# A fused adaLN block on one core: a new start-up order, another bound for the projection's scale, and operations that the planner deals between two engines

## The chip, the cores and the metric

The kernel runs on one core of one Trainium2 chip. TensorE (PE) multiplies, VectorE (DVE), ScalarE (ACT) and GpSimd (POOL) work on what it needs and leaves, and SyncE (SP) issues all the transfers from one queue. The metric is the time of one execution on the device, in microseconds (us). The program is the same each time; three executions of it are given below.

## The reference, cut to what matters

x is 2048 rows of 512. There are 32 heads of 128, and each query sees the last 512 rows of the cache (W), so that attention is over 512 keys for every one of the 2048 queries, without a mask.

```python
mod = (silu(c) @ w_mod).reshape(...)            # six vectors of 512: sa, ca, ga, sb, cb, gb
h = layernorm(x) * (1 + ca) + sa
q = h @ wq                                      # 32 heads of 128
p = softmax(q @ k.T * Dh ** -0.5)               # k, v: the last 512 rows of the cache
x = x + ga * ((p @ v) @ wo)
h = layernorm(x) * (1 + cb) + sb
x = x + gb * ((gelu(h @ w_gate) * (h @ w_up)) @ w_down)      # 512 -> 1376 -> 512
```

All inputs are float32.

## The kernel before, in words

**Precision.** Every large product is made of f16 matmuls. An operand is split in two f16 parts, high and low (`in_two`: ScalarE copies to f16, GpSimd subtracts that copy from the float32 value), and three products of 128x128 by 128x512 stand for one. So that the parts fit f16, each weight tile is multiplied by a power-like scale taken from its largest absolute value (`h_max`, then `cross_a` and `cross_b`, which bring eight such maxima across the partitions with a transpose and a small matmul and take a reciprocal), and the columns that scale and shift the first LayerNorm are multiplied by one factor (`cols_bound`, `cols_scale`), which `s_scale` takes out again in the softmax's scale.

**The work.** 16 groups of two heads, each with 4 blocks of 512 queries: 128 iterations of one head and one block (`slot`). An iteration makes scores `s_mm` (12 matmuls into `psS`), their row maxima `s_max` on VectorE, exponentials `s_exp` on ScalarE (into `p`, then an f16 copy `pp`), the low part `s_low` on GpSimd and its transposition by DMA (`pT`), the product with v `pv` (`psO`), its split `oT`, the product with wo (`psW`) and its addition into `acc`, in all 36 matmuls; the query projection (`psQ`) of a later iteration comes between. Beside that run the loads, scalings and splits of the next group's weights, and one time LayerNorm (`ln_stats`, `ln_norm`, then `chunk`: four transposes of 128x128 into PSUM, `ln1_split`: scale and shift, high part, low part). After the last group comes the feed-forward part; the last groups' iterations carry its first preparation (LayerNorm 2: `ln2_norm`, `ln2_chunk`, `ln2_high`, `ln2_low`; sums for a Strassen-like scheme: `f_full`, `f_sum`, `f_low`, `aw_sum`).

**The order.** Nothing is issued where it is written. A class `Weaver` stands in front of the engines: `note` records each operation with its engine, its planned duration and what it depends on, and `issue` then plans. It takes a due time for each operation from the order of the matmuls (`rank`), plays the program forward with a list scheduler (`play`: at each moment the engine that is free takes, among the operations that are ready, the one with the earliest due time), plays it backward for new due times (`back`), repeats this `TURNS` times, keeps the order with the earliest end and issues it. Each engine then works in that order and waits by semaphores for what its next operation needs. All instructions are issued from one line, `real(*a, **k)`, line 314; so nearly every instruction in the profile has L314, and only its tiles tell operations apart.

`play` also knows a port that GpSimd and VectorE have in common: each GpSimd operation, and each VectorE operation of the kind marked `lock` (a `tensor_scalar`, or one with two large operands in SBUF), holds it to its end. Each operation has one fixed engine, written into the code.

**The start.** `PLAN` lists by hand the steps of the start, and so the due times of the matmuls: those with -1 come before the first iteration, the others hang at halves of iterations. The loads are noted as x's first four tiles (`load_x(0)`), `wq` and `k` of head 0, `w_mod`'s two quarters-of-columns for the scale and the shift (`load_mod(1)`, `load_mod(0)`, four transfers of 256 KB each), then more of x and of the weights; the planner orders them. `stats`, `norm`, `turn0` and `chunk` make the first normalised block. `mod` (`mod_mm`, 4 matmuls with one column each for each of the 8 pieces of w_mod) makes the modulation columns in PSUM (`two`), `cols_add` adds them up, `cols_bound` takes

```python
nc.vector.tensor_tensor(sq, cols[:, 0:8], cols[:, 0:8], op=OP.mult)
nc.tensor.matmul(two[:, 0, 16:24], ones, sq, start=True, stop=True)
nc.vector.tensor_reduce(sc1[:, 2:3], two[:, 0, 16:24], op=OP.add, axis=AX.X)
```

and a power of -1/2 on GpSimd, `cols_scale` multiplies. `warm` (54, 0, 0, 2, 1, 16, 0 times) transposes the identity into a PSUM bank of its own (`warmed`, a `psQ`), with nothing read from it.

Of the kernel before, what the change touches and what calls it, by code (L numbers as in the profile page):

```python
# [17 lines left out]
P = 128  # L18
# [32 lines left out]
    (-1, "stats", 0, 0), (-1, "stats", 0, 1), (-1, "stats", 0, 2), (-1, "warm", 54), (-1, "stats", 0, 3),  # L51
    (-1, "mod", 1, 0), (-1, "mod", 1, 1), (-1, "max", "first", 0), (-1, "norm", 0, 2, "V"), (-1, "max", "first", 1),
    (-1, "mod", 1, 2), (-1, "cross", "first", "a"), (-1, "warm", 0), (-1, "mod", 1, 3), (-1, "norm", 0, 3, "V"),
    (-1, "warm", 0), (-1, "cross", "first", "b"), (-1, "mod", 0, 0), (-1, "high", "k", 0), (-1, "turn0", 3),
    (-1, "mod", 0, 1), (-1, "norm", 0, 1, "V"), (-1, "norm", 0, 0, "V"), (-1, "mod", 0, 2), (-1, "turn0", 2),
    (-1, "mod", 0, 3), (-1, "warm", 2), (-1, "low", "k", 0), (-1, "stats", 1, 0), (-1, "cols_add"),
    (-1, "cols_bound"), (-1, "stats", 1, 1), (-1, "turn0", 0), (-1, "high", "wq", 0), (-1, "cols_scale"),
    (-1, "s_scale"), (-1, "stats", 1, 2), (-1, "warm", 1), (-1, "scalars", 0, "qk"), (-1, "turn0", 1),
    (-1, "warm", 16), (-1, "low", "wq", 0), (-1, "max", "second", 1), (-1, "chunk", 0, 0, "", "S", "Y"),
    (-1, "max", "second", 0), (-1, "chunk", 0, 1, "", "S", "Y"), (-1, "warm", 0), (-1, "chunk", 0, 2, "", "V", "V"),  # L60
    (-1, "chunk", 0, 3, "", "S", "V"), (-1, "q", 0), (-1, "q_high", 0), (-1, "turn", 0), (-1, "stats", 1, 3),
# [24 lines left out]
class Weaver:  # L86


    LAG, DRAIN, LANES, TURNS = 60.0, 165.0, 8, 6
    NEXT = {"ACT": 95.0, "DVE": 85.0, "POOL": 45.0, "PE": 0.0, "SP": 0.0}  # L90

    def __init__(self, nc):
        self.nc = nc
        for name, engine in (("vector", "DVE"), ("scalar", "ACT"), ("gpsimd", "POOL"), ("tensor", "PE"), ("sync", "SP")):
            setattr(self, name, self.Port(self, engine, getattr(nc, name)))
        self.ops, self.held, self.seen, self.before, self.rings, self.table = [], {}, {}, {}, {}, {}
# [55 lines left out]

    def note(self, engine, what, real, a, k):
        op = len(self.ops)
# [4 lines left out]
        for x, write in [(x, False) for x in read] + [(x, True) for x in wrote]:  # L159
# [4 lines left out]
            if held is None:  # L164
                continue
# [23 lines left out]
        self.ops.append((engine, d, deps, real, a, k, n, lock))  # L189

    def rank(self):
# [18 lines left out]
        for engine, d, *_ in self.ops:  # L210
            at.append(t if engine == "PE" else 1e12)
            t += d if engine == "PE" else 0.0
# [7 lines left out]
    def play(self, at, users):  # L220
# [4 lines left out]
        can = {e: [] for e in self.NEXT}  # L225
        for n, op in enumerate(self.ops):
            if not op[2]:
                heapq.heappush(wait[op[0]], (0.0, n))
        free, landed, bus, shared, order = {e: 0.0 for e in self.NEXT}, [], 0.0, 0.0, []
        ends = [0.0] * len(self.ops)  # L230
        while len(order) < len(self.ops):
            t, e = min((max(free[e], 0.0 if can[e] else wait[e][0][0]), e) for e in free if can[e] or wait[e])
            while wait[e] and wait[e][0][0] <= t:
                n = heapq.heappop(wait[e])[1]
                heapq.heappush(can[e], (at[n], n))
            aside = []
            if e == "DVE" and shared > t + 100.0:
                while can[e] and self.ops[can[e][0][1]][7]:
                    aside.append(heapq.heappop(can[e]))
                if not can[e] and wait[e] and wait[e][0][0] < shared:  # L240
                    free[e] = wait[e][0][0]
            pick = None if aside and free[e] > t else heapq.heappop(can[e]) if can[e] else aside.pop(0)
            for x in aside:
                heapq.heappush(can[e], x)
            if pick is None:
                continue
            n = pick[1]
            order.append(n)
            d, size, lock = self.ops[n][1], self.ops[n][6], self.ops[n][7]
# [13 lines left out]
            for m in users[n]:  # L263
                ready[m] = max(ready[m], t + d if e == "PE" == self.ops[m][0] else end)
                left[m] -= 1
                if not left[m]:
                    heapq.heappush(wait[self.ops[m][0]], (ready[m], m))
        return order, ends

    def back(self, ends, users):  # L270
# [5 lines left out]
        for n, op in enumerate(self.ops):  # L276
            if not users[n]:
                heapq.heappush(wait[op[0]], (0.0, n))
        free, shared, done, at = {e: 0.0 for e in self.NEXT}, 0.0, 0, [0.0] * len(self.ops)
        while done < len(self.ops):  # L280
# [6 lines left out]
            d, size, lock = self.ops[n][1], self.ops[n][6], self.ops[n][7]  # L287
            if e == "SP":
                d = max(d, size)
# [5 lines left out]
            for m in self.ops[n][2]:  # L295
                f = self.ops[m][0]
# [3 lines left out]
                if not left[m]:  # L300
                    heapq.heappush(wait[self.ops[m][0]], (ready[m], m))
        return at

    def issue(self):
        at, users = self.rank()
        best = None
        for _ in range(self.TURNS):
            order, ends = self.play(at, users)
            if best is None or max(ends) < best[0]:
                best = max(ends), order  # L310
            at = self.back(ends, users)
        for n in best[1]:
            real, a, k = self.ops[n][3:6]
# [4 lines left out]
def adaln_block(ctx: ExitStack, tc: tile.TileContext, x, k_cache, v_cache, wq, wo,  # L318
# [83 lines left out]
    def ln_stats(key, src, j):  # L402
# [6 lines left out]
        if j == 3:  # L409
# [3 lines left out]
            if key != 0:  # L413
                nm = NMR[key] = small(base, 4, 4, "nmr")
                nc.gpsimd.tensor_tensor(nm, MV[key][:, :, 0], RS[key], op=OP.mult)
                nc.gpsimd.tensor_scalar(nm, nm, -1.0, 1.0, op0=OP.mult, op1=OP.mult)
# [70 lines left out]
    for h in range(G):  # L487
        load_raw("v", h)
        load_raw("wo", h)
    load_x(2)  # L490
    load_x(3)

# [17 lines left out]
    def h_gate(h):  # L510
        nc.gpsimd.tensor_tensor(RAW["wo", h], RAW["wo", h], ga, op=OP.mult)
# [103 lines left out]
    def a_sum(g, nm):  # L615
# [8 lines left out]
        nc.gpsimd.tensor_tensor(out, x, y, op=op)  # L624
# [4 lines left out]
    def t_full(p, c, nm, eng):  # L629
# [3 lines left out]
        eng.tensor_tensor(t, b[:, 0, c, :], b[:, 1, c, :], op=OP.add)  # L633

    def t_sum(p, c, out, x, y):
        nc.gpsimd.tensor_tensor(TF[p, c, out], TF[p, c, x], TF[p, c, y], op=OP.subtract)
# [155 lines left out]
    warmed = bank("psQ")  # L792


    def warm(n):
        for _ in range(n):
            nc.tensor.transpose(warmed[:, :P], ident, ident)

    def ln1_split(qg, c, full, low):
# [4 lines left out]
        if full is nc.scalar:  # L806
            nc.scalar.activation(f, pt, AF.Identity, scale=a, bias=b)
            nc.scalar.activation(dh, f, AF.Copy)
        else:
            nc.scalar.activation(dh, pt, AF.Identity, scale=a, bias=b)  # L810
            nc.vector.tensor_scalar(f, pt, a, b, op0=OP.mult, op1=OP.add)
        low.tensor_tensor(dl, f, dh, op=OP.subtract)
# [29 lines left out]
    sq = small(base, 8, 1, "sq")  # L842
# [795 lines left out]
```

## Time and profile before

| | us |
|---|---|
| median of 3 executions | 1701.87 |
| lowest, highest | 1700.04, 1704.01 |
| the execution that was profiled | 1702.24 |
| its span, first to last instruction | 1700.10 |
| its mean granted TensorE clock | 0.992 |
| TensorE busy | 1671.3 |
| VectorE, ScalarE, GpSimd busy | 1315.3, 1174.4, 1238.5 |

In the profile a row of a group reads: line, engine, operation, out <- in with the shapes, count, then busy time in all and nanoseconds of one, then the time that the engine stood idle just before, with what ended it. A row of the timeline reads: start, duration, engine, line, operation, out <- in, and in brackets the idle time ahead of it. A row of a stretch reads: from:to, its length, the busy time and count of each engine, the clock granted to TensorE (1.00 is full), the share of the DMA engines and GB/s. A float32 matmul of `mod_mm` leaves two records. Ends of matmuls are modelled: a 128x512 f16 matmul is shown with 380 ns, while in a dense run six of them start in 1.29 us.

### The profile page before, as it was taken

To read this page: it belongs to the slowest core of one execution; us is meant where nothing else is said; L and a number is where in the kernel's file an instruction comes from. 1 tells how busy PE (TensorE), PEld (TensorE's weight loads), DVE (VectorE), ACT (ScalarE), POOL (GpSimd) and SP (SyncE) were. 2 spreads that over 40 slices of the span, in tenths; PEclk is the share of its full clock that TensorE was granted. 3 is DMA by queue.
4 is the path that set the end of the run, shared out by engine and by line. 5 is a ranking of instruction groups with operands and counts; after the bars stand their busy time and mean duration, and the time that the engine had idled before them with its cause. 6 is when DMAs were issued, how large, how long until landed. Compare 5 with 4: busy or idle time off the path is not lost. (4 is left out here: it accounts for less than half of the span.)

```text
span 1700.1 us, 24167 instructions
## 1 busy us (share of the span) xinstructions
PE 1671.3 (98%) x7807; PEld 774.4 (46%) x7807; DVE 1315.3 (77%) x2423; ACT 1174.4 (69%) x2346; POOL 1238.5 (73%) x1033
## 2 busy tenths in 40 slices
PE   8899999999999999999999999999999999999998
PEld 6444444444444444444444444444444444444444
DVE  5887777788888777777777788888777888965665
ACT  3877777777777867777777776776777976654541
POOL 2899995878698868686777788897887786643630
PEclk7999999999999999999999999999999999999999
DMA  6777788799888878686777675787768711110011
GB/s 198 144 143 148 134 161 148 153 187 184 185 163 181 144 137 145 128 155 118 143 128 146 124 155 111 161 175 149 142 135 140 146 34 38 47 43 19 16 50 50
DMA packets 666351, 217.12 MB, mean 128 GB/s; under 512 B 581552, under 2 KB 648112, under 8 KB 666224
## 3 DMA queue, kind: packets, MB, share of 16 engines
q1 hardware_dynamic: 666224, 215.57, 63.8%
q8 instruction: 62, 1.02, 0.2%
q14 instruction: 65, 0.53, 0.1%
HBM read 68.68 MB, written 4.19 MB: 43 GB/s over the span
## 5 line engine op out<-in xcount | busy, mean ns | idle before, releaser
L314 POOL TENSOR_TENSOR pp<-p,pp 128x1024 f16<-128x1024 f32 x256 | 547.8, 2142 | 170.5 <-ACT pp L314 143.3
L314 ACT ACTIVATE p<-psS,st,es 128x512 f32<-128x512 f32 x512 | 393.2, 772 | 150.3 <-DVE st L314 129.1
L314 PE MATMUL psW<-wo,oT 128*128 128x512 f16 x1536 | 433.9, 380 | 0.3 <-DVE acc L314 0.2
L314 PE MATMUL psS<-kT,q 128*128 128x512 f16 x1536 | 418.6, 380 | 1.5 <-ACT q L314 1.3
L314 DVE SCALAR_TENSOR_TENSOR acc<-psW,st,acc 128x512 f32<-128x512 f32 x496 | 359.8, 743 | 53.6 <-PE psW L314 51.0
L314 PE MATMUL psO<-pT,v 128*128 128x512 f16 x1536 | 400.1, 379 | 0.5 <-DVE oT L314 0.5
L314 DVE TENSOR_REDUCE st<-psS 128x2 f32<-128x1024 f32 x256 | 312.0, 1219 | 79.1 <-PE psS L314 77.0
L314 ACT ACTIVATE pp<-p 128x1024 f16<-128x1024 f32 x256 | 269.8, 1054 | 10.3 <-DMA pT<-pp 5.5
L314 PEld LDWEIGHTS <-v 128*128 128x128 f16 x1536 | 150.4, 98 | 182.4 <-issue 1.9
L314 PEld LDWEIGHTS <-q 128*128 128x128 f16 x1536 | 149.8, 98 | 181.9 <-ACT q L314 4.1
L314 PEld LDWEIGHTS <-oT 128*128 128x128 f16 x1536 | 149.1, 98 | 176.6 <-issue 2.0
L314 DVE SCALAR_TENSOR_TENSOR oT<-psO,oT 128x512 f16<-128x512 f32 x128 | 87.7, 685 | 75.6 <-ACT oT L314 75.1
L314 PE MATMUL psQ<-B,A 128*128 128x512 f16 x528 | 144.2, 380 | 1.8 <-DVE A L314 1.8
L314 PEld LDWEIGHTS <-aw 128*128 128x128 f16 (+1 forms) x840 | 84.3, 100 | 96.7 <-issue 0.4
L314 PE MATMUL psQ<-T,S 128*128 128x512 f16 x468 | 115.4, 379 | 1.7 <-ACT h L314 1.7
L314 PEld LDWEIGHTS <-A 128*128 128x128 f16 x756 | 73.2, 98 | 96.2 <-issue 10.1
L314 PE MATMUL psS<-T,aw 128*128 128x512 f16 (+1 forms) x480 | 115.7, 379 | 0.0
L314 POOL TENSOR_SCALAR raw<-raw,av 128x512 f32<-128x512 f32 x122 | 85.1, 709 | 39.7 <-DVE av L314 27.5
L314 DVE TENSOR_REDUCE mx<-raw 128x1 f32<-128x512 f32 x128 | 85.9, 673 | 30.4 <-DMA raw<-in_A_v_cache_dram 18.3
L314 POOL TENSOR_TENSOR q<-h,q 128x512 f16<-128x512 f32 x78 | 90.6, 1162 | 19.3 <-ACT q L314 19.0
L314 ACT ACTIVATION_READ_ACCUMULATOR p<-psS,st,es 128x1 f32 x512 | 100.4, 196 | 0.0
L314 ACT ACTIVATE oT<-psO 128x512 f16<-128x512 f32 x128 | 75.6, 591 | 30.3 <-PE psO L314 29.9
(207 smaller groups left out, 2243.8 us busy)
## 6 DMA issues: line engine op xcount, KB each, us to landing
raw<-in_A_wq_dram SPq DMA_DIRECT2D x32, 256.0 KB, 3.4
raw<-in_A_k_cache_dram SPq DMA_DIRECT2D x32, 256.0 KB, 3.4
raw<-in_A_v_cache_dram SPq DMA_DIRECT2D x32, 256.0 KB, 3.4
raw<-in_A_wo_dram SPq DMA_DIRECT2D x32, 256.0 KB, 3.0
pT<-pp SPq DMA_TRANSPOSE x512, 3.3
raw<-in_B_w_gate_dram SPq DMA_DIRECT2D x24, 256.0 KB, 3.1
raw<-in_B_w_up_dram SPq DMA_DIRECT2D x24, 256.0 KB, 3.2
raw<-in_B_w_down_dram SPq DMA_DIRECT2D x20, 256.0 KB, 3.0
```

The costliest lines, as they stand in the source:

```text
L314: real(*a, **k)
```

## The change

1. **Loads.** x's first two groups of four tiles are noted first, then the two parts of w_mod, then k and wq of head 0, then the third group of x, and so on; and SyncE issues all of these in the order in which they are noted. Later loads are not planned sooner than 40 us (`EARLY`) before they are due.
2. **The scale.** `cols_bound` takes the sum of absolute values of the columns, in place of the sum of squares and its root: an upper bound of the same quantity, made with one column less work on TensorE and without GpSimd.
3. **Warming transposes.** 50 at the start, then 6 behind each of the eight modulation steps, now into the same PSUM tile as the modulation products (`two`).
4. **Dealing.** `either` records an operation with several possible engines, and `play` gives it to one: two-operand tensor operations (`tt`) to GpSimd or VectorE, scalings to GpSimd or ScalarE, norms and scale-and-shift from PSUM to ScalarE or VectorE. An engine leaves it if the other could end it sooner (`sooner`; a VectorE operation that needs the common port is charged `SHY` = 1500 ns more), and it also leaves any operation if one whose due time is over `WORTH` = 5000 ns earlier becomes ready before this one would be done (`pressing`).
5. **The planner.** It plans half clock for TensorE after a window of 3413 ns in which it is busy less than 35%, not counting one-column products, and takes 10 turns in place of 6.
6. The first LayerNorm also gets the column that ScalarE needs for a norm (`nmr`, two small GpSimd operations).

```diff
 PLAN = (
-    (-1, "stats", 0, 0), (-1, "stats", 0, 1), (-1, "stats", 0, 2), (-1, "warm", 54), (-1, "stats", 0, 3),
-    (-1, "mod", 1, 0), (-1, "mod", 1, 1), (-1, "max", "first", 0), (-1, "norm", 0, 2, "V"), (-1, "max", "first", 1),
...
+    (-1, "stats", 0, 0), (-1, "stats", 0, 1), (-1, "stats", 0, 2), (-1, "stats", 0, 3), (-1, "warm", 50), (-1, "mod", 1, 0), (-1, "warm", 6), (-1, "mod", 1, 1), (-1, "warm", 6),
+    (-1, "mod", 1, 2), (-1, "warm", 6), (-1, "mod", 1, 3), (-1, "warm", 6),
+    (-1, "mod", 0, 0), (-1, "warm", 6), (-1, "mod", 0, 1), (-1, "warm", 6),
+    (-1, "mod", 0, 2), (-1, "warm", 6), (-1, "mod", 0, 3), (-1, "warm", 6),
+    (-1, "cols_add"), (-1, "cols_bound"),
+    (-1, "max", "first", 0), (-1, "max", "first", 1), (-1, "cross", "first", "a"),
+    (-1, "cross", "first", "b"), (-1, "norm", 0, 0, "V"), (-1, "norm", 0, 1, "V"), (-1, "norm", 0, 2, "V"),
+    (-1, "norm", 0, 3, "V"), (-1, "turn0", 0), (-1, "turn0", 1), (-1, "turn0", 2), (-1, "turn0", 3),
+    (-1, "cols_scale"), (-1, "s_scale"), (-1, "high", "k", 0), (-1, "low", "k", 0), (-1, "high", "wq", 0),
...
-    LAG, DRAIN, LANES, TURNS = 60.0, 165.0, 8, 6
+    LAG, DRAIN, LANES, TURNS, SPAN, SHY, EARLY, WORTH = 60.0, 165.0, 8, 10, 3413.0, 1500.0, 40000.0, 5000.0
...
+        def arrive(n):
+            if span and n >= self.lead:
+                ready[n] = max(ready[n], span + at[n] - self.EARLY)
+            for e in self.ops[n][4]:
+                heapq.heappush(wait[e], (ready[n], n))
+
+        def sooner(n, e, t):
+
+            kinds = self.ops[n][4]
+            mine = max(t, shared if kinds[e][1] else 0.0) + kinds[e][0] + (e == "DVE" and kinds[e][1]) * self.SHY
+            for o, kind in kinds.items():
+                s = max(free[o], ready[n], shared if kind[1] else 0.0)
+                if o != e and s + kind[0] + (o == "DVE" and kind[1]) * self.SHY < mine:
+                    return max(s, t) + 1.0
+            return None
...
-                heapq.heappush(can[e], (at[n], n))
+                heapq.heappush(can[e], (n - 1e12 if e == "SP" and n < self.lead else at[n], n))
...
+            if e == "PE":
+                while t >= close:
+                    cold, work, close = work < 0.35 * self.SPAN, 0.0, close + self.SPAN
+                work += 0.0 if size == 1 else d
+                d *= 1.0 + cold
...
     load_x(0)
-    load_raw("wq", 0)
-    load_raw("k", 0)
+    load_x(1)
     load_mod(1)
     load_mod(0)
-    load_x(1)
+    load_raw("k", 0)
+    load_raw("wq", 0)
+    load_x(2)
     load_raw("wq", 1)
     load_raw("k", 1)
...
+    nc.lead = len(nc.ops)
...
     def h_scale(kind, h):
         raw = RAW[kind, h]
-        nc.gpsimd.tensor_scalar(raw, raw, AV[kind, h], 1.0, op0=OP.mult, op1=OP.mult)
+        av = AV[kind, h]
+        nc.either((nc.gpsimd, nc.scalar), lambda o: o.activation(raw, raw, AF.Copy, scale=av) if o is nc.scalar
+                  else o.tensor_scalar(raw, raw, av, 1.0, op0=OP.mult, op1=OP.mult))
 
     def in_two(t, src):
         nc.scalar.activation(t[:, 0, :], src, AF.Copy)
-        nc.gpsimd.tensor_tensor(t[:, 1, :], src, t[:, 0, :], op=OP.subtract)
+        tt(t[:, 1, :], src, t[:, 0, :], OP.subtract)
...
-    warmed = bank("psQ")
     def warm(n):
         for _ in range(n):
-            nc.tensor.transpose(warmed[:, :P], ident, ident)
+            nc.tensor.transpose(two[:, 1, :P], ident, ident)
+    crossing = bank("psQ")
+    def tt(out_, x_, y_, op, order=(nc.gpsimd, nc.vector)):
+        nc.either(order, lambda o: o.tensor_tensor(out_, x_, y_, op=op))
+
+    def affine(f, pt, a, b):
+        nc.either((nc.scalar, nc.vector), lambda o: o.activation(f, pt, AF.Identity, scale=a, bias=b) if o is nc.scalar
+                  else o.tensor_scalar(f, pt, a, b, op0=OP.mult, op1=OP.add))
...
-        nc.vector.tensor_tensor(sq, cols[:, 0:8], cols[:, 0:8], op=OP.mult)
+        nc.vector.tensor_reduce(sc1[:, 2:3], cols[:, 0:8], op=OP.add, axis=AX.X, apply_absolute_value=True)
     def cols_bound():
-        nc.tensor.matmul(two[:, 0, 16:24], ones, sq, start=True, stop=True)
-        nc.vector.tensor_reduce(sc1[:, 2:3], two[:, 0, 16:24], op=OP.add, axis=AX.X)
-        nc.vector.tensor_scalar(sc1[:, 3:4], sc1[:, 2:3], 1e-30, 2.0 / HQS ** 2, op0=OP.max, op1=OP.mult)
-        nc.gpsimd.tensor_tensor(sc1[:, 0:1], sc1[:, 3:4], eps_t[:, NC:NC + 1], op=OP.pow)
+        nc.tensor.matmul(two[:, 0, 16:17], ones, sc1[:, 2:3], start=True, stop=True)
+        nc.vector.tensor_scalar(sc1[:, 3:4], two[:, 0, 16:17], 1e-30, 1.0 / HQS, op0=OP.max, op1=OP.mult)
+        nc.vector.reciprocal(sc1[:, 0:1], sc1[:, 3:4])
...
     def acc_gate(t, eng):
-        eng.tensor_tensor(acc[t], acc[t], ga, op=OP.mult)
+        tt(acc[t], acc[t], ga, OP.mult)
...
     def ln2_low(qg, c, eng):
         hi, lo = f_view(qg, c)
         full = FULL.pop((qg, c)) if qg % 2 == 0 else FULL[qg, c]
-        eng.tensor_tensor(lo, full, hi, op=OP.subtract)
+        tt(lo, full, hi, OP.subtract)
```

The same replacement by `tt` stands in `h_gate`, `a_sum`, `t_full`, `t_sum`, `ln1_split`, `mod_mul`, `x_add`, `f_full`, `f_sum`, `f_low`, `wd_gate`, `plain_part`, and that of a scaling by `either` in `gu_scale` and `aw_scale`. `s_low`, `hid_low` and the sums `aw_sum` and `aw_low` of the feed-forward weights stay on their engines.

More of the change, by code (lines that the diff above doesn't have):

```diff
@@ L163, in note @@
             held = self.held.get(key)
-            if held is None:
+            if held is None or write and self.joins:
                 continue
@@ L266, in play, with back @@
                 if not left[m]:
-                    heapq.heappush(wait[self.ops[m][0]], (ready[m], m))
-        return order, ends
-    def back(self, ends, users):
+                    arrive(m)
+        return order, ends, by
+    def back(self, ends, by, users):
         import heapq
@@ L805, in ln1_split @@
         dh, dl = h_view(qg, c)
[L806 to L812, printed above, removed]
+        affine(f, pt, a, b)
+        nc.scalar.activation(dh, f, AF.Copy)
+        tt(dl, f, dh, OP.subtract)
     def ln1_turn(qg, c, where):
```

169 lines of the change are left out of this document (102 added, 67 removed).

## The prediction

> **What bounds the kernel now.** I read the page first, then busy time by stretches, the timeline of the first 40 us, what TensorE waited for, and the two places in the body where its busy time dips.
>
> ```profile
> span 1700.1 us, 24167 instructions
> ...
> PE 1671.3 (98%) x7807; PEld 774.4 (46%) x7807; DVE 1315.3 (77%) x2423; ACT 1174.4 (69%) x2346; POOL 1238.5 (73%) x1033
> ...
> 100.00:200.00 100.00, 100.00 (x466) 45.25 (x465) 74.16 (x148) 74.96 (x152) 99.17 (x77) 1.00 0.79 149
> ```
>
> TensorE is busy for 98% of the span at full clock, even between 100 and 200 us, where GpSimd (POOL) is busy for 99.17 of 100 us. No edit touches the products of attention or of the feed-forward part. So only time in which TensorE stands, or runs at half clock, can be won; nearly all of it lies in the first 70 us and at two places later.
>
> The start, from the timeline:
>
> ```profile
> 8.56 2.74 PE L314 MATMUL psS<-silu,wm 128*128 128x1 f32 x24
> ...
> 11.16 4.43 PE L314 MATMUL psQ<-ident 128*128 128x128 f32 x25
> ...
> 23.18 0.17 DVE L314 TENSOR_TENSOR cols<-psS,plus 128x8 f32<-128x8 f32 x1 [1.43 <-PE psS L314]
> ...
> 25.60 0.43 PE L314 MATMUL psS<-sq,ones 128*128 128x8 f32 x2
> ...
> 28.20 0.22 DVE L314 TENSOR_SCALAR cols<-cols,sc 128x8 f32<-128x8 f32 x1
> ...
> 28.51 0.78 ACT L314 ACTIVATE h<-psO,cols 128x512 f32<-128x512 f32 x1 [8.90 <-DVE cols L314]
> ...
> 37.42 1.24 PE L314 MATMUL psQ<-B,A 128*128 128x512 f16 x5
> ...
> 39.42 1.90 PE L314 MATMUL psS<-kT,q 128*128 128x512 f16 x8 [0.53 <-ACT q L314]
> ```
>
> The chain is: modulation products end, columns summed (23.18), a bound from their squares, columns scaled (28.20), four chunks of normalised x made (28.51 on), first projection done (38.66), first scores at 39.42. From 23.18 to 28.51 are 5.3 us of small steps, from 28.51 to 38.66 are 10.2 us for four chunks. The clock and DMA in the same stretch:
>
> ```profile
> 0.00:5.00 5.00, 3.65 (x17) 3.65 (x18) 1.10 (x4) 1.49 (x2) 1.35 (x16) 1.00 0.54 138
> 5.00:10.00 5.00, 5.00 (x46) 5.00 (x44) 1.08 (x2) 0.00 (x0) 0.00 (x0) 1.00 0.99 335
> ...
> 5.60:9.00 3.40, 3.40 (x34) 1.00 0.96 325
> 9.00:12.40 3.40, 3.40 (x32) 1.00 1.06 376
> 12.40:15.80 3.40, 3.40 (x18) 0.50 1.07 394
> 15.80:19.20 3.40, 2.94 (x26) 1.00 1.06 358
> 19.20:22.60 3.40, 3.40 (x19) 0.50 1.13 249
> ...
> 29.40:32.80 3.40, 0.94 (x2) 0.51 0.00 0
> 32.80:36.20 3.40, 3.40 (x12) 0.50 0.01 2
> ```
>
> (In the two 5 us rows the engines are PE, PEld, DVE, ACT, POOL; in the others PE alone; then clock, DMA share, GB/s.) The granted clock changes in steps of 3.4 us: a stretch of transposes (5.6 to 9.0) is followed by full clock, one of mostly one-column modulation products (9.0 to 12.4, 15.8 to 19.2) by half clock. The first real products, 29.4 to 36.2, run at half.
>
> **Part 1: the modulation chain.** New order of loads: c, 8 tiles of x, then w_mod. The two 5 us rows have moved 0.69 + 1.68 = 2.37 MB by 10 us; x's 8 tiles are 2.10 MB, so the first w_mod quarter lands at about 10.0 instead of before 8.56; the other seven follow at 0.7 us each, faster than they are used. Fifty warming transposes fill TensorE until about 9. Then eight steps of four products and six transposes, all in one PSUM tile, so in this order. Four products are 8 records: 2.74/24 x 8 = 0.91 us at full clock, 3.4/19 x 8 = 1.43 at half; six transposes 6 x 3.4/34 = 0.60, at half 6 x 3.4/18 = 1.13. A step is 1.51 or 2.56 us. All at full clock the eight take 12.1 us, and the 16 transposes of x 1.6 more: 10.1 + 13.7 = 23.8. All at half from 12.4 on: 1.5 steps done, 6.5 x 2.56 + 16 x 0.19 = 19.7, so 32.1. Transposes are 40% of a step; between 9.0 and 12.4 they were from 11.16 on, 1.2 of 3.4 us (36%), and that was not enough. I take one 3.4 us window at half (it costs 1.7): 25.5. Against 23.18 that is **+2.3** (ends +0.6 and +8.9).
>
> **Part 2: the scale.** The square, the 8-column matmul followed by a reduction, and the power on GpSimd become one absolute sum, a one-column matmul, one multiply and a reciprocal on VectorE. By the rows, 0.17 for each small step: 0.17 + 0.17 + 0.43 + 0.17 + 0.17 + 0.22, with a quarter microsecond of hand-overs, is 1.6 us, against 28.51 - 23.18 = 5.3: **-3.7**. The old chain also stood behind LayerNorm work in VectorE's and GpSimd's queues; that work now finds its x landed before it. If it comes back between the steps, 2 us of this go (end -1.7).
>
> **Part 3: the four chunks.**
>
> ```profile
> 28.72 0.20 POOL L314 TENSOR_TENSOR nmr<-mv,rs 128x4 f32<-128x4 f32 x1
> 29.01 0.27 POOL L314 TENSOR_SCALAR nmr<-nmr 128x4 f32<-128x4 f32 x1
> 31.23 1.16 POOL L314 TENSOR_TENSOR T<-h,T 128x512 f16<-128x512 f32 x1 [1.95 <-ACT T L314]
> ...
> L314 ACT ACTIVATE T<-h 128x512 f16<-128x512 f32 x3 | 1.8, 634 | 0.0
> ...
> 28.50:39.40 10.90, 7.03 (x30) 3.73 (x29) 9.33 (x26) 9.06 (x15) 6.67 (x11) 0.69 0.01 2
> ```
>
> VectorE and ScalarE were 9.33 and 9.06 of 10.9 us busy there, much of it with statistics, norms and maxima of later tiles. With x's first 8 tiles landed at 9.3 us this goes into their idle time ahead of the chunks. What is left: one affine (0.78), one f16 copy (0.63), then four subtractions on GpSimd, 4 x 1.16, and 0.4 for the last products: 6.4 us against 10.2: **-3.7** (ends 0 and -4.5). Two more GpSimd operations for the first LayerNorm (0.20 + 0.27 us) lie under the wait for w_mod; without that cover they cost 0.5.
>
> **Part 4: filling the pipeline.**
>
> ```profile
> 39.40:50.00 10.60, 7.89 (x36) 3.37 (x37) 9.41 (x23) 9.69 (x18) 6.16 (x7) 1.00 0.34 78
> 50.00:60.00 10.00, 7.26 (x32) 3.43 (x31) 8.60 (x17) 7.74 (x16) 9.67 (x9) 0.84 0.78 159
> 60.00:70.00 10.00, 8.41 (x42) 4.00 (x40) 8.97 (x17) 8.37 (x17) 6.13 (x6) 0.99 0.72 154
> ...
> PE psQ L314 <- DVE A L314: 1.8, 1, 1.8
> ...
> PE psO L314 <- DVE acc L314: 1.4, 1, 1.4
> ```
>
> TensorE idles 2.7 + 2.7 + 1.6 = 7.0 us, waiting for weight splits and for norms in VectorE's queue (the longest wait 1.8, the fourth 1.4). The 7.3 MB up to the last tile of x land by some 24 us at the 0.36 MB a us of the rows 9.0 to 19.2, so the norms can be done before. The exponentials and splits stay. I take half, **-3.5** (ends 0 and -7.0).
>
> **Part 5: the operations dealt out.** A two-operand subtraction may now go to GpSimd or VectorE. The planner's own sum charges VectorE 0.68 + 1.5 us (SHY) and GpSimd 1.16, and lets VectorE in only when the common port is free, which is when GpSimd is free too. So it deals all of them to GpSimd, VectorE's old ones among them:
>
> ```profile
> L314 DVE TENSOR_TENSOR T<-hf,T 128x512 f16<-128x512 f32 x12 | 19.8, 1660 | 1.9 <-ACT T L314 1.9
> ...
> L314 DVE TENSOR_TENSOR acc<-acc,ga 128x512 f32<-128x512 f32 x8 | 12.9, 1616 | 0.0
> ...
> L314 POOL TENSOR_TENSOR acc<-acc,ga 128x512 f32<-128x512 f32 x8 | 10.6, 1330 | 8.8 <-DVE iv L314 6.5 <-DVE acc L314 2.2
> ...
> 1038.15 6.60 DVE L314 TENSOR_TENSOR acc<-acc,ga 128x512 f32<-128x512 f32 x1
> ...
> 1374.44 7.05 DVE L314 TENSOR_TENSOR T<-hf,T 128x512 f16<-128x512 f32 x1 [1.92 <-ACT T L314]
> ...
> 1040.00:1050.00 10.00, 6.39 (x24) 2.39 (x23) 9.96 (x11) 2.49 (x6) 6.01 (x5) 0.83 0.56 105
> ...
> 1374.00:1388.00 14.00, 11.02 (x47) 4.81 (x46) 13.49 (x11) 9.90 (x18) 8.75 (x11) 0.88 0.13 39
> ...
> 1360.00:1400.00 40.00, 37.02 (x175) 17.66 (x174) 32.18 (x41) 29.46 (x52) 33.58 (x44) 0.96 0.13 37
> ...
> raw<-in_A_wq_dram SPq DMA_DIRECT2D x32, 256.0 KB, 3.4
> ```
>
> Two VectorE subtractions stretch to 6.60 and 7.05 us, while GpSimd works without a gap, and TensorE then stands 3.6 and 3.0 us and runs one 3.4 us window at half clock each: about 5.3 + 4.7 = 10 us. On GpSimd such an operation has its 1.3 us. But from 1360 to 1400 GpSimd is at 33.6 of 40 us, and some twelve moved operations bring 14 more; part of the delay returns there. I take half, **-5** (ends 0 and -10). Scalings that move to ScalarE, and loads held until 40 us before they are due, cost nothing: the first leaves GpSimd, the second has 40 us of cover for a landing of 3.4 us (the last row); without that cover each costs its landing.
>
> [...]
>
> **Sum**: +2.3 - 3.7 - 3.7 - 3.5 - 5 = -13.6. The profiled execution took 1702.24 us, its span 1700.10 and 2.14 around it; its median stands 0.4 below that. 1702.2 - 13.6 = 1688.6: **1689 us**.
>
> **Rivals.**
> *The chain stays at half clock* (0.18): 40% of transposes a window is not enough, as 36% was not. Columns at 32.1: +8.9 - 3.7 - 3.7 - 3.5 - 5 = -7.0, 1695; without the last two, 1704. For it: the 9.0 to 12.4 row; against: the row 5.6 to 9.0, where transposes alone are followed by full clock. [...]
> *More stretched subtractions* (0.10, the slower side): if subtractions do land on VectorE while GpSimd has no gap, as between 100 and 200 us, each stretched one costs TensorE about 5 us. The start's -8.6 is used up by the second; four give 1702.2 - 8.6 + 20 = 1714. Against it: the planner's arithmetic above.
> *The port moves, not the wait* (0.08): the term of part 5 is zero because GpSimd is late by as much. 1702.2 - 8.6 = 1694.
> *Nothing arrives* (0.06): GpSimd's and ScalarE's chunk work bounds the start whatever comes first, and part 5 gives nothing: 1702.
> *All of it* (0.08): chain at full clock, all of parts 4 and 5: +0.6 - 3.7 - 3.7 - 7 - 10 = -23.8, 1678.
>
> **How the numbers follow.** The forecast (0.50) has its own range, 1682 to 1696. The range, 1679 to 1704, leaves out the slower rival and part of the last. A measurement of this kernel can tell about 0.2%, 3.4 us. Faster by more: 0.50 + 0.08 + 0.08, and 0.09 of the half-clock rival: 0.75. Within: 0.06 and 0.07 of that rival: 0.13. Slower: 0.10 and 0.02 of it: 0.12.
>
> **What would show it.** Part 1: the columns' sum at 24 to 27 us; beyond 31 with clock 0.50 between is the half-clock rival. Part 2: under 2 us from there to the first affine. Part 3: first scores at 33 to 36 us. Part 4: fewer than 5 us of idle TensorE in the 30 us that follow. Part 5: no VectorE subtraction over 3 us in the body, and the dips near 1040 and 1380 smaller; GpSimd's busy time above 1238 less its scalings. A dip elsewhere, behind a late transpose of probabilities, would make the forecast wrong.

## The result and the profile after

| | median (lowest to highest), us | runs |
|---|---|---|
| before | 1702.52 (1698.98 to 1705.04) | 22 |
| after | 1708.72 (1697.92 to 1711.00) | 22 |

The ratio is 1.0032, 95% interval 1.0022 to 1.0041: the change makes the kernel 0.3% slower. The forecast was 13.6 us the other way. One thing is needed for the numbers below: the runs of after fall into two groups, three at 1697.9 to 1698.5 us and nineteen at 1705 to 1711; the profiled run, 1711.0, is of the second.

The head of the page of after:

```profile
span 1709.2 us, 24243 instructions
...
PE 1681.3 (98%) x7832; PEld 783.4 (46%) x7832; DVE 1279.6 (75%) x2366; ACT 1208.3 (71%) x2385; POOL 1269.2 (74%) x1051
```

TensorE is "98% busy" in both kernels; its busy time grew by 10 us for nearly the same work, at a mean granted clock of 0.987 in place of 0.992. GpSimd took 31 us more, VectorE 36 less. To see where the span grew by 9.1 us, I cut it at three marks: the first scores, and the first and last `oT`. The tile view of `oT` on ScalarE, before and then after (min/median/max ns of one, first to last start in us):

```profile
L314 ACT ACTIVATE oT<-psO x128: 574/591/637, 72.8 to 1367.5; 128x512 f16<-128x512 f32 x128
```

```profile
L385 ACT ACTIVATE oT<-psO x128: 573/597/612, 76.8 to 1367.2; 128x512 f16<-128x512 f32 x128
```

The first scores come at 45.87 in place of 39.42 us. So, stage by stage: to the first scores **+6.5**; from there to the first `oT` 30.9 in place of 33.4, **-2.5**; the body between first and last `oT` 1290.4 in place of 1294.7, **-4.3**; from the last `oT` to the end 342.0 in place of 332.6, **+9.4**. The sum is +9.1. Both losses must be explained, at the two ends of the program.

The start, in the timeline of after:

```profile
1.35 8.02 PE L385 MATMUL psS<-ident 128*128 128x128 f32 x50 [1.35 <-POOL eps_t L385]
...
11.50 1.02 PE L385 MATMUL psS<-silu,wm 128*128 128x1 f32 x8 [2.13 <-DMA wm<-in_w_mod_dram]
...
31.46 1.71 PE L385 MATMUL psS<-silu,wm 128*128 128x1 f32 x8
33.03 1.52 PE L385 MATMUL psS<-ident 128*128 128x128 f32 x6
...
34.55 1.49 PE L385 MATMUL psW<-ident,acc 128*128 128x128 f32 x6
...
34.66 0.17 DVE L385 TENSOR_TENSOR cols<-psS,plus 128x8 f32<-128x8 f32 x1 [10.81 <-PE psS L385]
...
36.30 0.16 DVE L385 TENSOR_SCALAR sc<-psS 128x1 f32<-128x1 f32 x1 [0.55 <-PE psS L385]
...
36.75 0.23 DVE L385 TENSOR_SCALAR cols<-cols,sc 128x8 f32<-128x8 f32 x1
...
37.08 0.81 DVE L385 TENSOR_SCALAR h<-psO,cols 128x512 f32<-128x512 f32 x1
...
45.87 1.03 PE L385 MATMUL psS<-kT,q 128*128 128x512 f16 x4
```

The first w_mod piece is awaited until 11.50, with TensorE idle for 2.13 us; a step late in the chain takes 1.57 for its products and 1.31 for its transposes, 2.88 us; the columns are summed at 34.66. Behind the sum, VectorE stands for 0.55 us (36.30) until the product of the bound is made, which comes in TensorE's order behind six transposes of x (34.55). The same stretch by windows (TensorE alone, then the clock):

```profile
5.60:9.00 3.40, 3.40 (x31) 1.00 1.00 361
9.00:12.40 3.40, 1.27 (x13) 1.00 1.07 384
12.40:15.80 3.40, 3.40 (x22) 0.59 1.06 380
...
32.80:36.20 3.40, 3.40 (x18) 0.50 0.01 2
36.20:39.60 3.40, 2.47 (x16) 0.89 0.00 0
```

The clock falls at about 13.0 us (0.59 in a window is full clock for 18% of it) and stays at 0.50 to the end of the chain.

The end, first the windows of after at the places of the two old dips and at the new ones (PE, PEld, VectorE, ScalarE, GpSimd; clock; DMA):

```profile
1040.00:1050.00 10.00, 10.00 (x49) 4.42 (x46) 9.15 (x18) 6.25 (x13) 9.48 (x7) 1.00 0.99 187
1374.00:1388.00 14.00, 14.00 (x66) 6.42 (x65) 12.21 (x9) 8.40 (x15) 14.00 (x14) 1.00 0.00 0
...
1390.00:1400.00 10.00, 5.88 (x19) 2.57 (x19) 6.21 (x9) 4.54 (x7) 1.46 (x2) 0.66 0.00 0
1420.00:1430.00 10.00, 4.38 (x19) 1.78 (x18) 9.29 (x8) 5.54 (x11) 6.08 (x8) 0.81 0.28 79
```

Both old dips are full now: 10.00 of 10 us against 6.39, 14.00 of 14 against 11.02. Two new ones stand at 1390 and 1420, deeper and again with a lower clock. What lies in them, in the timeline of after:

```profile
1379.76 0.67 POOL L385 TENSOR_TENSOR aw<-S3f,aw 128x256 f16<-128x256 f32 x1
...
1379.80 12.21 DVE L385 TENSOR_TENSOR hid<-r,hid 128x512 f16<-128x512 f32 x1
...
1389.21 2.26 POOL L385 TENSOR_TENSOR T<-hf,T 128x512 f16<-128x512 f32 x2
...
1392.54 0.74 DVE L385 SCALAR_TENSOR_TENSOR r<-psS,ffs,r 128x512 f32<-128x512 f32 x1
...
1393.33 0.58 PE L385 MATMUL psS<-B,aw 128*128 128x512 f16 x1 [5.30 <-DVE r L385]
...
1393.97 0.69 DVE L385 TENSOR_TENSOR hid<-r,hid 128x512 f16<-128x512 f32 x1 [0.69 <-ACT hid L385]
...
1416.81 7.59 DVE L385 SCALAR_TENSOR_TENSOR r<-r,ffs 128x512 f32<-128x512 f32 x1
...
1423.17 0.67 POOL L385 TENSOR_TENSOR aw<-raw,aw 128x256 f16<-128x256 f32 x1
...
1428.93 1.44 PE L385 MATMUL psS<-B,aw 128*128 128x512 f16 x3 [5.62 <-DVE r L385]
```

One `hid_low`, an operation that the change left on VectorE, lasts from 1379.80 to 1392.01, 12.21 us; undisturbed, one takes 0.69 (1393.97). GpSimd issues one operation behind the other up to 1391.47, and about 0.55 us after that the `hid_low` is done. Behind it in VectorE's queue, and behind a second `hid_low` of ordinary length, stands the `r` (1392.54) for which TensorE waits 5.30 us. The same again at 1416.81: an operation of VectorE with both operands in SBUF, 7.59 us, GpSimd without a gap up to 1423.84, the end about 0.55 us after that, and a wait of 5.62 us for an `r` soon behind.

### The profile page after: what moved, and what is told of

Same layout as the page of the kernel before. It is cut to its first block, busy times and chain, and to the rows that moved or that the text cites. A ratio compares the mean times of both kernels' runs of the same rounds, so it can differ in the third digit from the quotient of the medians.

```text
span 1709.2 us, 24243 instructions
## 1 busy us (share of the span) xinstructions
PE 1681.3 (98%) x7832; PEld 783.4 (46%) x7832; DVE 1279.6 (75%) x2366; ACT 1208.3 (71%) x2385; POOL 1269.2 (74%) x1051
## 4 chain that ended last, share of the span: by engine, by line
PE 92%; DVE 3%; ACT 2%; issue 1%; DMA 1%; POOL 1%; SPq 0%; DVEq 0%; ACTq 0%; POOLq 0%
PE psS L385 30%; PE psW L385 23%; PE psO L385 21%; PE psQ L385 17%; DVE r L385 1%; DVE st L385 1%; DVE acc L385 1%; ACT p L385 0%; ACT T L385 0%; DMA wm<-in_w_mod_dram 0%; POOL pp L385 0%; DMA pT<-pp 0%; SPq L385 0%; ACT pp L385 0%; ACT h L385 0%
## 5 line engine op out<-in xcount | busy, mean ns | idle before, releaser
L385 PE MATMUL psO<-pT,v 128*128 128x512 f16 x1536 | 406.4, 380 | 0.0
L385 POOL TENSOR_TENSOR q<-h,q 128x512 f16<-128x512 f32 x78 | 90.9, 1165 | 24.2 <-ACT q L385 23.9
L385 PE MATMUL psS<-B,aw 128*128 128x512 f16 (+1 forms) x360 | 90.9, 390 | 11.6 <-DVE r L385 11.5
```

## The experiments

Each kernel is after with one edit, or with two that were first run alone. In most of them the order that the planner found is kept and the edit acts only where it is issued, so that nothing else moves; the line that issues becomes

```diff
-            real, a, k = self.ops[n][4][best[2][n]][2:]
-            real(*a, **k)
+            real, a, k = self.ops[n][4][self.force.get(n, best[2][n])][2:]
+            for _ in range(self.times.get(n, 1)):
+                real(*a, **k)
```

The warming transposes' results are read by nothing, so leaving them out or doubling them changes no output. Here are all runs together (before was run beside each); the marks are those of the profiled run.

| kernel | median (lowest to highest), us | ratio to before, 95% | columns summed | last `oT` to end |
|---|---|---|---|---|
| after | 1708.7 (1697.9 to 1711.0) | 1.0032 (1.0022 to 1.0041) | 34.7 | 342.0 |
| no transposes between products | 1699.1 (1697.2 to 1700.4) | 0.9984 (0.9976 to 0.9993) | 23.9 | 341.7 |
| twelve per step | 1705.5 (1699.4 to 1712.5) | 1.0016 (1.0003 to 1.0030) | 30.5 | 342.0 |
| feed-forward sums on VectorE | 1687.7 (1681.2 to 1694.5) | 0.9916 (0.9891 to 0.9940) | 24.1 | 327.2 |
| `hid_low` on GpSimd | 1699.2 (1694.0 to 1702.1) | 0.9984 (0.9974 to 0.9994) | 33.6 | 333.5 |
| 70 at the start | 1698.5 (1696.9 to 1703.6) | 0.9982 (0.9973 to 0.9990) | 29.3 | 341.3 |
| 70 at the start, sums on VectorE | 1683.1 (1682.2 to 1684.3) | 0.9889 (0.9875 to 0.9903) | 24.2 | 327.2 |
| new start alone | 1690.7 (1683.8 to 1695.7) | 0.9930 (0.9908 to 0.9953) | 23.9 | 328.4 |
| dealing alone | 1690.7 (1689.3 to 1694.0) | 0.9937 (0.9925 to 0.9949) | 23.1 | 335.3 |
| no transposes between, sums on VectorE | 1684.8 (1683.9 to 1687.3) | 0.9901 (0.9884 to 0.9917) | 23.8 | 327.2 |
| 30 at the start, sums on VectorE | 1696.1 (1696.0 to 1698.1) | 0.9967 (0.9954 to 0.9980) | 34.8 | 327.3 |

### No transposes between the products

```diff
         for _ in range(n):
+            if n == 6:
+                nc.times[len(nc.ops)] = 0
             nc.tensor.transpose(two[:, 1, :P], ident, ident)
```

> The changed kernel with the eight groups of six transposes between the modulation products left out where instructions are issued; every other instruction in the same order. Theory A (the start is lost to transposes that run at half clock and do not lift it): the columns' sum moves from 34.7 us to about 24 to 25 us (eight groups of 1.31 us less), first scores from 45.9 to about 36 to 38, the whole 7 to 10 us less than the changed kernel, about 1700. Rival B (the start is not what costs, the feed-forward part is): the start moves as said, but the time stays within 2 us of the changed kernel, since later stages wait for something else.

The 48 transposes cost more than they bring: without them the sum comes at 23.9 us although the clock is half from 12.4 to 29. The windows of this kernel:

```profile
9.00:12.40 3.40, 2.04 (x18) 0.97 1.06 371
12.40:15.80 3.40, 3.40 (x18) 0.50 1.06 386
```

After minus this run is 9.6 us, nearly the 10.7 by which the sum is earlier. The last stage is the old 341.7: the end's loss has another cause.

### Twelve per step

The edit is the same with 2 in place of 0.

> The changed kernel with each of the transposes between the modulation products issued twice, 12 per step in place of 6. Theory A (a window counts by its share of transposes, and 45% was too little): with some 60% the granted clock goes to 1.00 within one or two windows, steps take 2.2 us in place of 2.9, the columns' sum comes at 30 to 33 us and the first products run at full clock; 3 to 5 us less than the changed kernel, and its times lie closer together. Rival B (transposes in this place cannot lift the clock whatever their number): each step takes 4.1 us, the sum comes at about 44 us and the time rises by 8 to 10 us.

The windows:

```profile
9.00:12.40 3.40, 1.66 (x11) 0.85 1.06 367
12.40:15.80 3.40, 3.40 (x23) 0.65 1.06 384
15.80:19.20 3.40, 3.40 (x35) 1.00 1.07 365
```

The clock falls at about 11.4 (0.85), is back at about 14.8 and then holds. So transposes, enough of them, do win it back; but a step with twelve takes 2.2 us at full clock, and the median is only 3.2 us better than after. The times did not come closer together, as expected: they spread over 13 us.

### Feed-forward sums back on VectorE

```diff
         tt(lo, full, hi, OP.subtract)                       # ln2_low
+        if qg:
+            nc.force[len(nc.ops) - 1] = "DVE"
```

and the same for `f_full`, `f_sum` with n = 1 and `f_low`: the operations that stood on VectorE before.

> The changed kernel in its own order, but the two-operand operations that prepare the feed-forward part (low parts of LayerNorm 2 from the second block on, and the sums and low parts of the Strassen-like scheme that were on VectorE before) are issued on VectorE again. Theory C (GpSimd without a gap shuts VectorE's own two-operand operations out of the common port): GpSimd gets gaps between 1360 and 1480 us, VectorE's stretch of 12.8 us at 1380 falls under 6 us, and from the last split of attention's output to the end it takes 333 to 337 us in place of 342; 1700 to 1704. Rival D (the order of the planned work is what is late, whatever the engine): that stage stays at 340 to 345 us.

The last stage falls from 342.0 to 327.2 us, more than expected, and 5.4 less than before's own 332.6. Its windows, without a dip:

```profile
1360.00:1400.00 40.00, 39.72 (x198) 19.45 (x197) 35.47 (x50) 30.38 (x55) 25.00 (x26) 1.00 0.05 14
1400.00:1440.00 40.00, 39.95 (x187) 18.23 (x186) 34.29 (x42) 23.63 (x48) 27.10 (x28) 1.00 0.20 56
```

GpSimd is busy for 25.00 of 40 us here, and no VectorE operation lasts over 3 us between 1340 and 1480. The runs are again in two groups, three at 1681.2 to 1683.5 and three at 1691.9 to 1694.5, the profile in the first, with its chain at full clock. The mean clock is 0.997 to 1.000 in the first three and 0.989 to 0.993 in the others; with the end mended, this points to the start as what parts the groups.

### `hid_low` on GpSimd

```diff
+        nc.other[len(nc.ops) - 1] = nc.nc.gpsimd.tensor_tensor   # hid_low
```

(`other` holds the call that is issued in place of the planned one.)

> The changed kernel in its own order, but the subtraction for the low part of the hidden layer (VectorE before and after) is issued on GpSimd. Theory C (port): the stretched VectorE operation at 1380 is gone and TensorE's wait of 5.3 us at 1393 with it, though GpSimd gets 1.2 us of work for each block; the stretched multiplication at 1417 stays; the last stage takes 336 to 340 us in place of 342. Rival E (GpSimd simply has too much to do there): with still more on GpSimd the last stage gets longer than 342 us.

The 12.21 us are gone, the last stage is 8.5 us shorter. That GpSimd simply has too much to do is not the cause: it has more to do here (40.00 us from 1360 to 1400, 31.46 in after), and the stage is shorter. But GpSimd is fuller still, and the next two-operand operations of VectorE take the wait. Window and timeline of this kernel:

```profile
1360.00:1400.00 40.00, 38.32 (x189) 18.39 (x186) 20.21 (x30) 28.66 (x49) 40.00 (x44) 1.00 0.10 27
```

```profile
1406.26 3.42 DVE L387 SCALAR_TENSOR_TENSOR r<-r,ffs 128x512 f32<-128x512 f32 x2
1434.03 5.14 DVE L387 SCALAR_TENSOR_TENSOR r<-r,ffs 128x512 f32<-128x512 f32 x2
```

### Seventy transposes at the start, alone and with the sums on VectorE

```diff
+            if n == 50 and i < 20:
+                nc.times[len(nc.ops)] = 2
```

> The changed kernel in its own order, with 70 in place of 50 transposes at the start, so that TensorE works until about 11.5 us, when the first piece of w_mod lands, and does not stand 2.1 us in the window from 9.0 to 12.4 us. Theory F (that idle gap makes the window too empty, the clock falls to half, and six transposes a step are enough to hold full clock but not to win it back): the clock is 1.00 from 5.6 to 23 us in the profile, a step takes 1.5 us, the columns' sum is at 24 to 26 us, and the times lie in one group near the lowest of the changed kernel, 1698 to 1700. Rival A (six transposes a step are too few at any clock): still half clock from about 16 us on, sum at 32 to 36 us, 1707 to 1711.

> 70 transposes at the start, and the operations that prepare the feed-forward part issued on VectorE as before; the rest as changed. If the two losses are separate, they add: about 1682 to 1685 in one group, under the kernel before by 1.0 to 1.2%. If they share a cause, no better than the better mode of the run with the old engines alone, and spread over 1682 to 1694.

With the idle time before w_mod filled, the times go to the lower group of after: eleven of twelve runs from 1696.9 to 1702.0, median 1698.5, with the last stage unchanged. The profiled run is the slowest of the twelve, and it lost the clock later, at 19.2. Here are the transposes alone (all instructions that read the identity), first of this run, then of the kernel with both edits:

```profile
12.40:15.80 3.40, 2.05 (x16) 1.00 1.07 380
15.80:19.20 3.40, 1.48 (x12) 1.00 1.07 363
19.20:22.60 3.40, 2.04 (x10) 0.50 1.09 358
```

```profile
12.40:15.80 3.40, 1.72 (x13) 1.00 1.06 385
15.80:19.20 3.40, 1.81 (x15) 1.00 1.08 364
```

1.48 us of transposes in 3.4 were followed by half clock, 1.72 were not. This is no sharp bound: behind the chain of the kernel with both edits, from 24.65 to 28.07, there are 1.9 us of transposes, TensorE is busy for only 2.2, and half clock follows. A step at full clock, in the timeline of the kernel with both edits, is 1.50 us, of which the transposes have 0.69 (12.78 to 13.47):

```profile
11.97 0.95 PE L387 MATMUL psS<-silu,wm 128*128 128x1 f32 x8
12.78 0.85 PE L387 MATMUL psS<-ident 128*128 128x128 f32 x6
13.47 0.95 PE L387 MATMUL psS<-silu,wm 128*128 128x1 f32 x8
```
With both edits the four runs lie within 2.1 us, at 1683: this version beats both kernels, before by 1.1%. The two gains add: 10.2 us from the start and 14.8 from the end make 25.0; measured, 25.6.

### No transposes between, sums on VectorE; thirty at the start, sums on VectorE

> The run without the 48 transposes between the modulation products and the run with the feed-forward sums back on VectorE, in one kernel. Theory A and C together (two separate losses, one of the start and one of the port): the columns' sum at about 24 us at half clock, as without the transposes, first scores near 35, the last stage near 327 us as with the sums on VectorE; 1699 less 15 = 1684 to 1687 us, in one group of times, since no clock has to be held. If the gain of the last stage came only with a start at full clock: 1699, the last stage near 341. If the two overlap: between 1690 and 1697.

> Thirty opening transposes in place of fifty, six per step kept, the feed-forward sums back on VectorE. Theory F (the gap ahead of the first w_mod piece drops the clock, and six transposes per half-clock step don't win it back): TensorE now stands some 4 to 5 us before the first modulation product, so that the half clock comes in every run; columns' sum at 33 to 36 us, first scores at 44 to 47, one group of times at 1691 to 1696 us, none near 1682. If the clock follows the share of transposes in the steps alone (theory A without the gap): the steps are the same, so as with seventy, 24 us and 1683. If the two groups have nothing to do with the gap: times in two groups 10 us apart, 1682 and 1692, as with fifty.

The first gave 1684.8 in one group, as the two separate losses say. The second is the reverse test of the idle time: its timeline and windows,

```profile
1.35 5.09 PE L387 MATMUL psS<-ident 128*128 128x128 f32 x30 [1.35 <-POOL eps_t L387]
10.85 1.25 PE L387 MATMUL psS<-silu,wm 128*128 128x1 f32 x8 [4.40 <-DMA wm<-in_w_mod_dram]
```

```profile
9.00:12.40 3.40, 1.55 (x10) 0.87 1.07 382
12.40:15.80 3.40, 3.40 (x19) 0.50 1.07 375
...
22.60:26.00 3.40, 3.40 (x19) 0.50 0.27 67
```

show 4.40 us idle and half clock from about 11.5 to the chain's end; sum at 34.8; five runs in one group at 1696.0 to 1698.1, none near 1683. The steps are those of the kernel with seventy, transpose for transpose; only the opening transposes, and with them the idle time ahead of the steps, differ, and 13 us follow.

The other traces fit. With six transposes a step, TensorE stood for 0.71 us ahead of the first product in the kernel with the sums on VectorE, and not at all in the one with both edits: the clock held through the chain. It stood for 1.56 us with `hid_low` on GpSimd, for 2.13 in after and for 4.40 with thirty: half clock by the second step. With seventy alone it did not stand there, and the clock fell only in the fifth step, behind a short wait for w_mod.

### The new start alone, and the dealing alone

Both were planned anew, by the new planner, so that more than the edit moves. In the first every operation has its engine of before; in the second `PLAN`, loads, squares and warming are those of before.

> The new loads, scale, warming transposes and planner, but nothing dealt: each operation on its engine of before; planned anew. By what the runs so far show: the start as in the changed kernel (columns' sum at 34 us, or 24 where the clock holds), the stage from the last split of attention's output to the end 328 to 335 us in place of 342, and the port's stretched gating operation near 1040 may come back. 1693 to 1702. If dealing as such, not what it does to the end, is what costs, the body shows it too: under 1690.

> The start of before (its plan, loads, squares and transposes), with the new planner and the dealing; planned anew. Expected: the start as before (sum at 23 to 24 us, first scores at 38 to 40), attention's body 4 us shorter, the stage from the last split to the end as in the changed kernel, 338 to 343 us: 1702 to 1706. If the dealing is harmless by itself and only the late start pushes the end together, the last stage takes under 335 us and the time is under 1698.

Both came out faster than expected, at 1690.7. Each half makes the kernel 0.6 to 0.7% faster, and the whole makes it slower. The start alone shows the two groups again (1683.8 to 1687.8, 1693.6 to 1695.7). In it both stretched operations of before are gone, although nothing is dealt; two of its groups, to be compared with 1660 and 1616 ns in the prediction's rows of before, and a window:

```profile
L385 DVE TENSOR_TENSOR T<-hf,T 128x512 f16<-128x512 f32 x12 | 13.7, 1148 | 0.0
...
L385 DVE TENSOR_TENSOR acc<-acc,ga 128x512 f32<-128x512 f32 x8 | 9.4, 1189 | 0.0
...
1374.00:1388.00 14.00, 13.24 (x68) 6.60 (x65) 13.66 (x14) 13.11 (x24) 14.00 (x11) 1.00 0.15 37
```

No VectorE operation of this kernel takes over 2.5 us. The body from the first to the last `oT` takes 1287.8 us in place of before's 1294.7, the last stage 328.4 in place of 332.6. So the new order, with no operation dealt, is enough to remove both old stretches. The window shows more: GpSimd has no gap from 1374 to 1388 here either (14.00 us), but fourteen operations of VectorE and eleven of GpSimd get through in these 14 us, and two of VectorE's, at 1377.71 and 1382.16, take 1.16 us, some 0.45 longer than undisturbed (0.69). Why VectorE gets through here and is done only behind the end of the run in after is open.

In the dealing alone a VectorE operation stretches at the same place as in after, but for less; timeline of that kernel:

```profile
1367.38 10.25 DVE L383 TENSOR_TENSOR hid<-r,hid 128x512 f16<-128x512 f32 x1
```

Its first scores come at 34.3 us, with before's own scale and chain; from the columns' sum (23.12) to the first affine (25.55) it takes 2.4 us, as long as after with the new scale. So an earlier first score doesn't need the new scale: the new planner and the dealing do it as well, and what of -2.9 and -2.1 (below) each edit is worth can't be told from these runs.

## Why the prediction was wrong, by its own steps

**Part 1, forecast +2.3, measured +11.5: the failed step at the start.** "I take one 3.4 us window at half" stood between ends of +0.6 and +8.9. In the traces with fifty opening transposes and six per step there is nothing between: the chain runs at full clock throughout (sums on VectorE) or, from its second step, at half (after). At full clock 0.69 us of transposes in a step of 1.50 are 1.56 in a 3.4 us window: near the edge, since 1.48 lost it and 1.72 held it. Once it is lost, the step takes 2.88 us, and a window holds 7 transposes in place of 14 (3.4/2.88 and 3.4/1.50 steps of six): they didn't win it back, and twelve per step did. The prediction compared shares of time (36% and 40%) and missed that at half clock the share stays the same (1.31 us of 2.88 at half, 0.69 of 1.50 at full, 45 and 46%) while the work halves, 7 transposes for 14.

What tips it is the arrival: w_mod forecast at 10.0 and met at 11.50, with TensorE idle in between. 4.40 us idle gave half clock (five runs in one group, one of them traced), filling it gave full clock through the chain in the profile with both edits, and fifty transposes gave either. The half-clock rival had been given 0.18 and the columns at 32.1; by their times it held in nineteen of 22 runs, with 34.7 in the one that was traced. That is beyond the term's end of +8.9, because the products begin 1.5 us late and a step at half clock takes 2.88 us where 2.56 were reckoned; against that, only five of the sixteen transposes of x that the sum counts stand ahead of the columns. That the three runs at 1698 are those at full clock is inferred from the same two groups in the kernel with the sums on VectorE (profile at full clock, 1683.5) and from their mean clock, 0.994 against 0.986 to 0.990; none of the three was traced.

The clock falls at 11.4, 11.5, 13.0 and 19.2 us in these traces. More transposes do bring it back: twelve per step took it from half to 1.00 (0.65 in the window from 12.4, 1.00 in the next). The planner's rule for half clock is shown by no run: 1.48 us of transposes in 3.4 (44%, more than it asks for) were followed by half clock. Why the first product starts at 10.38 us in one trace (sums on VectorE) and at 11.50 in another (after), with the same start, is not shown.

**Part 2, forecast -3.7, measured -2.9** (34.66 to 37.08, 2.4 us). What is missing is mostly the half clock again: the product of the bound waited behind six transposes of x at half clock, while at full clock (sums on VectorE, 24.06 to 25.76) the step takes 1.7 us, near the 1.6 of the forecast. That the new scale is what gained the time is not shown: the dealing alone keeps the old one and takes 2.4 us as well.

**Part 3, forecast -3.7, measured -2.1** (first affine to first scores, 8.8 in place of 10.9). VectorE works without a gap from 37.08 to 41.8 us, and between its affines it has four maxima and splits of weights there, 2.8 us; the prediction took only the chunks' own work.

**Part 4, forecast -3.5, measured -2.5.** Right in sign, and a third smaller. TensorE's idle time in the 30 us behind the first scores fell from 7.0 to 2.9 us.

**Part 5, forecast -5, measured -4.3 in the body and +9.4 at the end: the other failed step.** Both old stretched subtractions are gone. But the credit that the prediction gave to the dealing is not shown: in the new start alone, with nothing dealt, they are gone too, and the body is shorter still (1287.8 us). That the body's -4.3 lies near the forecast is, for the dealing, luck.

The error at the end is in "part of the delay returns there. I take half". The prediction counted 14 us more on a GpSimd with 6 us free, and priced it as GpSimd's own lateness. It did not ask which two-operand operations of VectorE were *not* dealt out (`hid_low`, `r`), and what a gapless GpSimd does to them: here they were done only 0.55 us behind the end of the whole run, after 7.59 and 12.21 us, and TensorE waited for what was queued behind them. So the term at the end was not a gain but a loss of 9.4; with the operations that prepare the feed-forward part back on VectorE, and everything else in the same order, the stage is 14.8 us shorter, in each of four kernels that have this edit (327.2 to 327.3). The prediction had the warning in its own words: both old stretched operations stood "while GpSimd works without a gap". Of its rivals, "more stretched subtractions" (0.10) had the loss, about 5 us of TensorE for each (5.30 and 5.62 here), but asked for dealt operations to land on VectorE; the ones that stretched had never been dealt.

The common port that the planner reckons with is not shown by the traces; they show times. In after `hid_low` was not done when the GpSimd instruction under way was (0.67 us, at 1379.76), but only 0.55 us behind the end of the whole run of them (1391.47).

**The sum.** -13.6 was forecast, +9.1 came (spans): +9.2 at part 1, +0.8, +1.6 and +1.0 at parts 2 to 4, and +10.1 at part 5, where the forecast's -5 meets +5.1. Two rivals held at once, half clock and stretched operations, which the list had only one by one. Even the three runs at 1698 are 4 us ahead of before, not 13.6. Shown by the runs: where both losses come from, and that they add. Open: how much of parts 2 to 4, and of the body, belongs to which edit, what the dealing is worth beside the new planner, and why the dealing alone, planned anew, loses less at the end (335.3) than the whole (342.0).

## What to carry to other kernels

A warming pattern between short steps must be counted as work per 3.4 us at half clock as well. Here six transposes a step held full clock in two traces (sums on VectorE, alone and with seventy; 14 in 3.4 us) and did not win it back at half (7 in 3.4 us): one idle gap of 2.13 us in after went before a whole stage at 0.50, and the run times split in groups. Before moving two-operand operations from VectorE to GpSimd, list those that stay behind and look for stretches in which GpSimd would have no gap: there they may be done only behind the end of its run, as at two places of after (12.21 and 7.59 us), or get through with less delay, as in the start alone (1.16 us for 0.69); only the trace tells which. And where a term's two ends are two states of a switch, take one of them, not the middle.

## What was not expected of the hardware

- One idle stretch of 2 to 4 us ahead of the chain costs 10 to 13 us behind it (1708.7 against 1698.5 us with fifty and seventy opening transposes; 1696 against 1683 with thirty and seventy and the sums on VectorE).
- A VectorE operation of 0.69 us took 12.21 us beside back-to-back GpSimd operations, and ended 0.55 us after the last of them. Sixteen two-operand operations of VectorE last over 2.4 us in the twelve traces; the four of before and after (6.60, 7.05, 12.21 and 7.59 us) all end 0.55 us after the last GpSimd operation of such a run (1044.20, 1380.94, 1391.47, 1423.84). Yet in the new start alone fourteen VectorE operations got through in 14 us without a gap on GpSimd.
- A chain of one-column products without any transposes between is as early at half clock (23.9) as with six per step at full clock (23.9 to 24.2): the transposes take the time that the clock gives.
